# Gated linear attention with a gated projection: 64-token halves with stacked heads, a packed state, and a convolution on TensorE for two of six chunks

## The chip, the cores and the metric

The kernel runs on one core of one Trainium2 chip. Its time is the device time of one execution in microseconds (us), and a smaller number is better. TensorE (PE) multiplies matrices into PSUM; the profile lists its weight loads apart, as PEld. VectorE (DVE), ScalarE (ACT) and GpSimd (POOL) do the elementwise work. SyncE (SP) issues the transfers. PSUM has eight banks, each of 512 float32 on every one of 128 partitions.

## The reference

Two stages follow each other. The first is a linear attention with a decay of its own for each channel, with batch 4, 8 heads, 768 tokens and head dimension 48. The second is a causal convolution with 5 taps over the result, a sigmoid of it as a gate, and two projections of 384 by 384.

```python
f = 1.0 / (1.0 + np.exp(-f_logit))
for t in range(S):
    state = f[:, :, t, :, None] * state + np.einsum('bhd,bhe->bhde', k[:, :, t], v[:, :, t])
    y[:, :, t] = np.einsum('bhd,bhde->bhe', q[:, :, t], state)
# x = y with the heads side by side: [4, 768, 384]
for k in range(5):
    gate_pre += conv_w[k][None, None, :] * xp[:, k:k + S, :]    # xp: x after four rows of zeros
out = (1 / (1 + np.exp(-gate_pre))) * (x @ w_val) @ w_out
```

## The kernel before

The 768 tokens are cut into six chunks of 128. Two heads make a pair, which lies on partitions 0 to 47 and 64 to 111, with channels on partitions and tokens along the free dimension; 4 batches times 4 pairs are 16 columns ("bp") of a chunk.

For each chunk, `pexp` and `pln` (ACT) make the negative logarithm of the decay, `scan` (DVE) sums it along the chunk, and `exp1` and `exp2` (ACT) give the decay products E1 and their inverses E2. `pmulq` and `pmulk` (DVE) scale q and k by them. Then, per batch:

- `scores` (line 282): products of k and q, 128 by 128 tokens for each of eight heads, into the PSUM tile `aps`.
- `mask` (line 289): DVE multiplies all of `aps` with a triangle of ones, 128 by 1024 elements, into `asb`.
- `ktrans` and `kevac`: PE transposes k, and ACT copies it to `ksb`.
- `apply` (line 302): y of one batch into `xps`, from the state and q and from v and the masked scores. The output is split into strips of 32 channels, which run side by side on four strips of the array.
- `xevac`: ACT copies y into `XF`, behind the last four tokens of the chunk before (`halo`).
- `dstate`: the products of k and v, into `dps`. Per half of the batches `stadd` (DVE) adds them to the state, `stmul` (POOL) multiplies it with the decay over the chunk, and `stcopy` (ACT, two copies) writes it as two blocks of a diagonal into `st`, which `apply` reads.

For each chunk's projections, `msplit` (ACT) and `mlow` (DVE) split y into two parts of reduced precision. `mlast` (ACT) multiplies y with the fifth tap, and four `mconv` steps (DVE) per block of 128 channels add the other taps, each over 128 by 512 elements. `gate` (ACT) is the sigmoid. `mval` (nine products per block) makes x times w_val, `mmul` (DVE) multiplies with the gate, `mhigh` (ACT) and `mrest` (DVE) split the product, `mout` (nine products) makes the output, and `mstore` copies and stores it. The last chunk's projections are done as two halves of the batches, numbered 5 and 6.

The weights come as 64-bit numbers. `weight` rebuilds float32 from their bits on POOL, ACT and DVE, in several steps each.

The order of the work is written out by hand: `PROGRAM` (lines 37 to 100) lists the pieces, and each engine does its instructions in the order in which they are written (class `Ordered`, line 103). Loads and stores go through SP's queue in the order of the program; a load whose buffer is still being read waits there, and everything behind it waits too. "busy" pieces are products of zeros that nobody reads. After the program a flag tells whether every chunk's decay stayed in range; if not, a general branch does everything anew. It isn't taken here.

In the profile nearly all instructions have line 113, since `Ordered` issues them; the groups are told apart by their tiles. `mps` are the projections' two PSUM banks, `e` the decay products, `gt` the gate, and `rg` and `re` are buffers used again for parts of projections' operands.

Of the kernel before, what the change touches and what calls it, by code (L numbers as in the profile page):

```python
# [21 lines left out]
C = 128  # L22
NC = S // C
BP = B * NP
KT = 5
HALO = KT - 1
NM = DM // 128
#: a chunk's decay products have to stay above this for q * e and k / e to be formed apart
RANGE = 2.0**-58
# [3 lines left out]
WHOLE = [(0, BP)]  # L33
# [3 lines left out]
PROGRAM = """  # L37
halo 0; loadf 0 0; loadf 0 1; busy 10; loadq 0 1; loadq 0 0; loadk 0 0; loadv 0 0; pexp 0 0; loadk 0 1; loadq 0 2;
pln 0 0; loadf 1 0; scan 0 0; loadv 0 1; pexp 0 1; busy 4; loadk 0 2; exp2 0 0; pln 0 1; wload 0; exp1 0 0; busy 4;
loadk 1 0; pmulk 0 0; pexp 0 2; loadq 1 0; pmulq 0 0; ktrans 0 0; loadv 0 2; scan 0 1; pln 0 2; scores 0 0; exp2 0 1;  # L40
scan 0 2; wload 1; exp1 0 1; busy 4; kevac 0 0; pmulq 0 1; exp2 0 2; dstate 0 0; pmulk 0 1; busy 4; exp1 0 2;
mask 0 0; loadv 1 0; ktrans 0 1; loadf 2 0; okc 0; kevac 0 1; pmulq 0 2; scores 0 1; pexp 1 0; weight 0; pmulk 0 2;
apply 0 0; pln 1 0; mask 0 1; loadf 3 0; loadk 2 0; dstate 0 1; wload 2; ktrans 0 2; scores 0 2; kevac 0 2; scan 1 0;
xevac 0 0; stadd 0 0; exp2 1 0; ktrans 0 3; mask 0 2; apply 0 1; kevac 0 3; pmulk 1 0; scores 0 3; stcopy 0 0;
scan 1 1; xevac 0 1; exp1 1 0; ktrans 1 0; loadk 2 1; mask 0 3; apply 0 2; exp2 1 1; loadq 2 0; pmulq 1 0; exp1 1 1;
apply 0 3; loadv 2 0; weight 1; weight 0; xevac 0 2; weight 0; pmulq 1 1; scores 1 0; xevac 0 3; weight 1; halo 1;
msplit 0; weight 1; loadq 2 1; weight 1; dstate 0 2; mask 1 0; dstate 0 3; kevac 1 0; ktrans 1 1; weight 0; stadd 0 1;
scores 1 1; kevac 1 1; pmulk 1 1; loadv 2 1; pexp 2 0; weight 0; weight 1; dstate 1 1; weight 1; apply 1 0; okc 1;
mask 1 1; weight 1; loadf 4 0; pln 2 0; weight 1; mlow 0; weight 3; ktrans 1 2; loadk 3 0; scores 1 2; xevac 1 0;
stcopy 0 1; scan 2 0; apply 1 1; mask 1 2; exp2 2 0; exp1 2 0; weight 0; scan 2 1; weight 2; scores 1 3; loadq 3 0;  # L50
mlast 0 0; pmulk 2 0; xevac 1 1; weight 2; exp2 2 1; mconv 0 0 0; dstate 1 0; mask 1 3; apply 1 2; loadv 3 0;
kevac 1 2; exp1 2 1; pmulq 2 0; ktrans 1 3; pmulq 2 1; scores 2 0; loadk 3 1; kevac 1 3; xevac 1 2; mconv 0 0 1;
weight 3; mlast 0 1; stadd 1 0; ktrans 2 0; weight 2; mlast 0 2; dstate 1 2; stmul 1 0; weight 3; dstate 1 3;
weight 3; stcopy 1 0; apply 1 3; weight 2; mask 2 0; kevac 2 0; stadd 1 1; okc 2; scores 2 1; loadv 3 1; weight 2;
xevac 1 3; stmul 1 1; pmulk 2 1; loadq 3 1; stcopy 1 1; mconv 0 2 0; ktrans 2 1; pexp 3 0; dstate 2 0; loadk 4 0;
weight 2; apply 2 0; weight 3; mask 2 1; kevac 2 1; loadf 5 0; weight 2; mconv 0 1 0; pln 3 0; dstate 2 1; weight 2;
mconv 0 1 1; ktrans 2 2; apply 2 1; weight 4; mconv 0 1 2; kevac 2 2; stadd 2 0; weight 3; stmul 2 0; mconv 0 0 2;
weight 3; dstate 2 2; loadq 4 0; stcopy 2 0; scan 3 0; weight 3; scores 2 2; loadv 4 0; weight 5; mconv 0 0 3;
exp2 3 0; mval 0 0; mconv 0 1 3; gate 0 0; mconv 0 2 1; mconv 0 2 2; mval 0 1; mask 2 2; exp1 3 0; mmul 0 0;
ktrans 2 3; scan 3 1; mval 0 2; weight 4; weight 4; exp2 3 1; mconv 0 2 3; exp1 3 1; scores 2 3; pmulq 3 0; halo 2;  # L60
xevac 2 0; pmulk 3 0; kevac 2 3; gate 0 2; apply 2 2; loadk 4 1; mask 2 3; pmulq 3 1; xevac 2 1; dstate 2 3; weight 5;
gate 0 1; scores 3 0; weight 5; xevac 2 2; stadd 2 1; weight 5; stmul 2 1; weight 4; ktrans 3 0; weight 4; apply 2 3;
pexp 4 0; mask 3 0; weight 4; pmulk 3 1; scores 3 1; loadv 4 1; loadq 4 1; mmul 0 1; kevac 3 0; mmul 0 2; weight 4;
ktrans 3 1; pln 4 0; weight 5; weight 4; dstate 3 0; loadk 5 0; weight 5; apply 3 0; mask 3 1; weight 6; weight 5;
scan 4 0; weight 5; weight 6; scores 3 2; kevac 3 1; weight 6; xevac 2 3; exp2 4 0; weight 6; weight 6; apply 3 1;
exp1 4 0; weight 6; mask 3 2; mhigh 0 1; mhigh 0 0; mrest 0 1; dstate 3 1; loadq 5 0; weight 6; mrest 0 0; scores 3 3;
mhigh 0 2; loadv 5 0; weight 6; mlast 1 0; mrest 0 2; mlast 1 1; pmulk 4 0; mout 0 1; msplit 1; mconv 1 0 0;
# [577 lines left out]
```

## Time and profile before

| what | value |
|---|---|
| median of 3 runs | 220.92 us (220.72 to 226.4) |
| span of the profiled execution | 227.6 us |
| ACT busy in that span | 144.0 us, 63% |
| POOL busy in that span | 32.4 us, 14% |
| moved by transfers | 29.54 MB, 130 GB/s on average |
| granted TensorE clock, mean | 0.921 of full |

The profiled execution's span runs from its first to its last instruction. It is 6.7 us longer than the median of the runs.

In a group's row, the line, the engine and the operation come first, then what it writes and reads, its shapes and the number of instructions; behind the bar stand the busy time in us, the mean duration of one in ns, and the engine's idle time just before these instructions, with what ended it. Instructions of one engine overlap a little, so busy time divided by the count is somewhat less than the mean of one. A float32 product is two instructions on TensorE, and each of them has a weight load.

In a row of the timeline or of the chain, the start and the length are in us from the span's start, and merged instructions are counted at the end. The length of merged products includes the whole of the last one, and products overlap.

### The profile page before, as it was taken

The numbers are of one execution on the slowest core, as the hardware profiler recorded it, in microseconds if no ns is written. First come the engines' busy times: TensorE is split into PE (matmuls) and PEld (weight loads), VectorE is DVE, ScalarE is ACT, GpSimd is POOL, SyncE is SP. The second block draws the span as 40 slices with busy tenths as digits, with TensorE's granted clock in tenths as the row PEclk, the third lists the DMA queues.
The fourth block names the chain that finished last, engine by engine and source line by source line (L and its number), as shares of the span: only waits on it lengthen the run. The fifth ranks groups of instructions, "written<-read, shape, count | busy, mean of one in ns | idle before, by whom it ended". The sixth has DMA issues, their size and how long they took to land.

```text
span 227.6 us, 5654 instructions
## 1 busy us (share of the span) xinstructions
PE 184.2 (81%) x2437; PEld 148.5 (65%) x2438; DVE 191.7 (84%) x251; ACT 144.0 (63%) x226; POOL 32.4 (14%) x37
## 2 busy tenths in 40 slices
PE   7298689649198847775999987979879999999990
PEld 3156568438087736665787875767867788889880
DVE  5395989497499999999997999997799999998800
ACT  4677764686249298967639998553941858553630
POOL 4001011200044842240115100001200000000000
PEclk9959959976979999998599999979999999999998
DMA  6999999999959902244023050120000012111241
GB/s 190 280 254 268 333 336 278 238 239 258 240 129 278 250 15 84 81 164 143 21 92 128 3 164 0 49 95 0 4 3 0 1 49 79 62 50 42 103 152 37
DMA packets 9183, 29.54 MB, mean 130 GB/s; under 512 B 1200, under 2 KB 2224, under 8 KB 8112
## 3 DMA queue, kind: packets, MB, share of 16 engines
q1 hardware_dynamic: 9152, 29.12, 44.5%
q8 instruction: 21, 0.34, 0.6%
q14 instruction: 10, 0.08, 0.1%
HBM read 24.39 MB, written 4.72 MB: 128 GB/s over the span
## 4 chain that ended last, share of the span: by engine, by line
DVE 33%; PE 27%; DMA 24%; ACT 9%; issue 3%; SPq 2%; DVEq 0%; ACTq 0%
PE mps L113 19%; DMA qb<-in_q 10%; DVE gt L113 10%; DMA vb<-in_v 9%; DVE e L113 6%; DMA fb<-in_f 5%; DVE asb L113 5%; ACT e L113 3%; PE aps L113 3%; DVE qb L113 2%; DVE cb L113 2%; PE xps L113 2%; DVE ca L113 2%; DVE kb L113 2%; SPq L178 2%
## 5 line engine op out<-in xcount | busy, mean ns | idle before, releaser
L113 ACT ACTIVATE e<-e 112x1024 f32<-112x1024 f32 (+3 forms) x40 | 39.9, 1003 | 15.0 <-DVE e L113 14.6
L113 DVE SCALAR_TENSOR_TENSOR gt<-xf,cws,gt 128x512 f32<-128x512 f32 x60 | 45.2, 772 | 0.6
L113 PE MATMUL aps<-qb,kb 48*128 48x128 f32 x384 | 31.5, 310 | 13.3 <-DVE asb L113 11.9
L113 PE MATMUL xps<-asb,vb 128*32 128x128 f32 x768 | 38.2, 293 | 1.1 <-DMA vb<-in_v 0.7
L113 PEld LDWEIGHTS aps<-qb,kb 48*128 48x128 f32 x384 | 26.6, 210 | 19.0 <-DVE asb L113 14.2
L113 PE MATMUL xps<-qb,st 112*32 112x128 f32 x480 | 31.7, 287 | 4.7 <-issue 2.9
L113 PEld LDWEIGHTS xps<-asb,vb 128*32 128x32 f32 x768 | 32.8, 119 | 2.6 <-DMA vb<-in_v 1.0
L113 DVE TENSOR_TENSOR_SCAN e<-keep,e 112x1024 f32<-112x1024 bf16 (+1 forms) x13 | 28.7, 2218 | 5.2 <-ACT e L113 5.0
L113 PE MATMUL mps<-rg,woH 128*128 128x512 f32 (+1 forms) x102 | 32.3, 401 | 0.3 <-DVE gt L113 0.3
L113 DVE TENSOR_TENSOR asb<-aps,tri 128x1024 f32<-128x1024 f32 x24 | 29.1, 1213 | 0.0
L113 PEld LDWEIGHTS xps<-qb,st 112*32 112x32 f32 x480 | 22.2, 114 | 7.4 <-issue 3.9
L113 PEld LDWEIGHTS mps<-rg,woH 128*128 128x128 f32 x102 | 19.1, 199 | 4.6 <-DVE gt L113 0.5
L113 PE MATMUL mps<-xH,wvH 128*128 128x512 f32 x45 | 19.2, 428 | 3.1 <-DVE gt L113 2.9
L113 PE MATMUL mps<-rg,woL 128*128 128x512 f32 (+1 forms) x51 | 20.1, 395 | 0.0
L113 DVE TENSOR_TENSOR kb<-kb,e 112x1024 f32<-112x1024 f32 (+1 forms) x13 | 15.4, 1184 | 5.2 <-DMA kb<-in_k 5.2
L113 PE MATMUL mps<-xL,wvH 128*128 128x512 f32 x45 | 18.5, 410 | 0.9 <-DVE xL L113 0.9
L351 POOL TENSOR_TENSOR ss<-u,e 112x384 f32<-112x384 f32 x8 | 9.4, 1173 | 67.2 <-DVE u L113 63.3
L113 DVE TENSOR_TENSOR qb<-qb,e 112x1024 f32<-112x1024 f32 (+1 forms) x13 | 14.7, 1130 | 4.6 <-DMA qb<-in_q 4.6
L113 PE MATMUL mps<-xH,wvL 128*128 128x512 f32 x45 | 18.5, 411 | 0.0
L113 PE MATMUL dps<-vb,ksb 128*48 128x48 f32 x320 | 11.7, 226 | 7.6 <-DVE u L113 5.1
L113 PEld LDWEIGHTS dps<-vb,ksb 128*48 128x48 f32 x320 | 9.7, 137 | 11.5 <-DVE u L113 5.3
L113 ACT ACTIVATE e<-fb 112x2048 f32<-112x2048 f32 (+2 forms) x8 | 11.8, 1481 | 8.3 <-DMA fb<-in_f 8.2
(107 smaller groups left out, 301.8 us busy)
## 6 DMA issues: line engine op xcount, KB each, us to landing
fb<-in_f SPq DMA_DIRECT2D x5, 896.0 KB, 19.1
qb<-in_q SPq DMA_DIRECT2D x9, 448.0 KB, 8.1
kb<-in_k SPq DMA_DIRECT2D x9, 448.0 KB, 11.6
vb<-in_v SPq DMA_DIRECT2D x9, 448.0 KB, 9.4
out<-osb SPq DMA_DIRECT2D x15, 256.0 KB, 2.0
raww<-in_wv SPq DMA_DIRECT2D x1, 1152.0 KB, 19.8
raww<-in_wo SPq DMA_DIRECT2D x1, 1152.0 KB, 26.7
kb<-in_k SPq DMA_DIRECT2D x1, 896.0 KB, 13.5
```

Of the source, the lines that this page charges most:

```text
L113: ins = emit(*a, **kw)
L178: nc.sync.dma_start(dst[c % NB][: src.shape[1], x0:x1], src[c, :, x0:x1])
L351: nc.gpsimd.tensor_tensor(out=ss[:, HS[h]], in0=U[h][:], in1=decay(c, h), op=ALU.mult)
```

## The change

The layout of a chunk's attention changes, the state is kept in another form, the convolution of two chunks moves to TensorE, and the whole order is new.

- **Halves.** A chunk of 128 tokens is handled as two halves of 64 (u = 0, 1). Scores are made only inside each half, as 64 by 64 squares. What the second half takes from the first comes through a state at the middle of the chunk (`MID`). Pieces work on two batches at a time (h = 0, 1), so there are 12 of each kind for 24.
- **Stacked heads.** The two heads of a pair have their tokens on different halves of the 128 partitions: masked scores, transposed k and v hold one head's 64 tokens on partitions 0 to 63 and the other's on 64 to 127. v is laid out with 160 columns for 112, with zeros between, and the inputs have 128 partitions for 112.
- **Packed state.** The state holds 64 columns per pair: for one head, and for the other, the parts that go to a shared strip of 32 channels lie in the same columns. `stmid` adds the first half's products to it (DVE, out of PSUM), and `stend` the second half's; `stmul` multiplies in place. `stadd` and `stcopy` go.
- **PSUM.** Six banks are three pairs that transposes, states, scores and y take in turn; when none of these is left to come, the banks pass to the projections.
- **Four taps in one product.** For chunks 3 and 4, `xload` copies y into `X4`, 32 channels at a time, four times, each shifted by one token; `mfour` multiplies with a matrix of four diagonals, and `mfifth` adds the fifth tap out of PSUM. `mlast` and `mconv` of those chunks go.
- **Loads.** f is loaded straight into E1, where `pexp` works in place; the buffers `fb` go. Stores are pieces of their own (`out`).

The diff, cut to its core:

```diff
-    qb = [mp.tile([112, BP, C], F32, name=f"qb{i}") for i in range(NB)]
-    vb = [mp.tile([C, BP, 112], F32, name=f"vb{i}") for i in range(NB)]
+    qb = [mp.tile([128, BP, C], F32, name=f"qb{i}") for i in range(NB)]
+    vb = [mp.tile([C, BP, VA + VB], F32, name=f"vb{i}", tag=f"vb{i}") for i in range(NB)]
+    pairs = [ps.tile([128, 2, 512], F32, name=f"pair{i}") for i in range(3)]
...
+    for t in pairs:
+        DVE.memset(t[32:64], 0.0)
...
+            DVE.tensor_tensor(out=W4[:].rearrange("p m g i -> p (m g) i"),
+                              in0=diag[:].unsqueeze(1).to_broadcast([128, 4 * NM, 32]),
+                              in1=cws[:, NM * KT :].unsqueeze(2).to_broadcast([128, 4 * NM, 32]), op=ALU.mult)
...
     def pexp(c, x0, x1, n):
-        act(LNEXP, E1[c % NB][:112, x0:x1], fb[c % NB][:112, x0:x1], AF.Exp, scale=-1.0, accum_out=sums[:, c, n : n + 1])
+        e = E1[c % NB][:112, x0:x1]
+        act(LNEXP, e, e, AF.Exp, scale=-1.0, accum_out=sums[:, c, n : n + 1])
...
+    def pair(*key):
+        held[key] = spare.pop(0)
+        uses[0] -= 1
+        return held[key]
+
+    def done(*key):
+        spare.append(held.pop(key))
+        while len(spare) > uses[0]:
+            t = spare.pop(0)
+            free.extend([t[:, 0], t[:, 1]])
+
+    def ktrans(c, h):
+        t = pair("k", c, h)
+        for i in range(HP + 1):
+            for s in range(2):
+                at = h * KH + (i * C if s == 0 else i % HP * C + HC)
+                PE.transpose(t[:, s, i * D : i * D + D], kb[c % NB][rows(s), at : at + C], ident[rows(s), rows(s)])
+
+    def dstate(c, h):
+        t, ks = pair("d", c, h), KSB[slot(c, h)]
+        for i in range(HP):
+            vt = vb[c % NB][:, h * HP + i]
+            for u in range(2 if c < NC - 1 else 1):
+                for s in range(2):
+                    r = slice(HC, C) if s == u else slice(0, HC)
...
+                    PE.matmul(t[rows(s), u, i * HC : i * HC + HC], ks[r, s, i + (u if s == 0 else 0)], vr, start=True,
+                              stop=True, tile_position=(r.start, s * HC))
+
+    def stmid(c, h):
+        t = held["d", c, h][:112, 0].rearrange("p (a e) -> p a e", e=HC)
+        DVE.tensor_tensor(out=MID[:, HS[h]], in0=ST[c % 2][:, HS[h]], in1=t, op=ALU.add)
...
+    def stend(c, h):
+        t = held["d", c, h][:112, 1].rearrange("p (a e) -> p a e", e=HC)
+        DVE.tensor_tensor(out=ST[(c + 1) % 2][:, HS[h]], in0=MID[:, HS[h]], in1=t, op=ALU.add)
+        done("d", c, h)
+
+    def stmul(c, h):
+        s = ST[(c + 1) % 2][:, HS[h]]
+        nc.gpsimd.tensor_tensor(out=s, in0=s, in1=E1[c % NB][:112, HS[h], C - 1 : C].to_broadcast([112, HP, HC]),
+                                op=ALU.mult)
+
+    def scores(c, h):
+        t, qt = pair("s", c, h), qb[c % NB]
+        kt = kview(c, h * HP, (h + 1) * HP)
+        for i in range(HP):
+            for u in range(2):
+                w = slice(u * HC, u * HC + HC)
+                for s in range(2):
+                    at = HC if s == u else 0
+                    PE.matmul(t[at : at + HC, u, i * HC : i * HC + HC], kt[rows(s), i, w],
+                              qt[rows(s), h * HP + i, w], start=True, stop=True, tile_position=(s * 64, at))
+
+    def mask(c, h):
+        DVE.tensor_tensor(out=ASB[slot(c, h)][:], in0=held["s", c, h][:].rearrange("p u (a t) -> p u a t", t=HC),
+                          in1=tri[:].unsqueeze(1).unsqueeze(1).to_broadcast([C, 2, HP, HC]), op=ALU.mult)
+        done("s", c, h)
+
+    def apply(c, h):
+        t, qt, at_, st, vt = pair("x", c, h), qb[c % NB], ASB[slot(c, h)], ST[c % 2], vb[c % NB]
...
+                    for s in range(2):
+                        if n == "s":
+                            r = rows(s)
+                            lhs, rhs = (MID if u else st)[r, bp, 32:64], qt[r, bp, w]
+                        else:
+                            r = slice(s * HC, s * HC + HC)
+                            lhs, rhs = vt[r, bp, VA + 32 :], at_[r, 1, i]
+                        PE.matmul(to(b, 2 * s, u, z), lhs, rhs, start=(b == 0 and kind == (("s", 0 if c else 1))),
+                                  stop=False, tile_position=(s * HC, z * 32))
...
+                ops = [(1, 0, st[:, bp, 0:32], qt[:112, bp, 0:HC])] if c else []
+                ops += [(1, 1, MID[:, bp, 0:32], qt[:112, bp, HC:]), (1, 1, vt[:, bp, VA : VA + 32], at_[:, 1, i])]
+                ops += [(g, 0, vt[:, bp, at : at + 32], at_[:, 0, i]) for g, at in ((0, 32), (1, 0), (2, 64))]
...
+                    PE.matmul(to(b, g, u, z), lhs, rhs, start=False, stop=(b == 1 and n >= -1), tile_position=(0, z * 32))
...
+    def xload(n, j):
+        src = XF[n % 2]
+        size = B * TH - j
+        for g in range(4):
+            nc.sync.dma_start(X4[j * 32 : j * 32 + 32, :, g].rearrange("p m b t -> p m (b t)")[:, :, 0:size],
+                              src[g * 32 : g * 32 + 32].rearrange("p m b t -> p m (b t)")[:, :, j:])
+
+    def mfour(w, m, bank):
+        w["pc", m] = bank
+        for g in range(4):
+            PE.matmul(bank[g * 32 : g * 32 + 32, : w["n"]], W4[:, m, g], X4[:, m, g, w["b"], 0:C], start=True, stop=True,
+                      tile_position=(0, g * 32))
+
+    def mfifth(w, m):
+        DVE.scalar_tensor_tensor(out=w["gt"][:, m], in0=w["xf"][:, m, w["b"], HALO:],
+                                 scalar=cws[:, m * KT + HALO : m * KT + KT],
+                                 in1=w["pc", m][:, : w["n"]].rearrange("p (b t) -> p b t", t=C), op0=ALU.mult, op1=ALU.add)
```

Of the new order, the loads of the start and the pieces behind the last mask are those that the prediction speaks of. The loads come as `loadf 0 0; wload 0; loadf 0 1; loadf 1 0; loadk 0 2; wload 1; loadk 0 1; loadk 0 0; loadq 0 0; loadv 0 1; loadv 0 2; loadq 0 1; loadq 0 2; loadv 0 0; wload 2; loadq 1 1; loadq 1 0; loadk 1 1; loadk 1 0; loadf 2 0; loadk 2 0; loadv 1 1; loadk 3 1; loadv 2 1; loadk 2 1; loadq 2 0; loadv 1 0`. Behind `mask 5 1` PE has `mval 3` (two blocks), `mval 5 1`, `apply 5 1`, `mfour 4` (three), and then the other products of `mout 3`, `mval 4`, `mval 5`, `mout 5`, `mval 6`, `mout 4` and `mout 6`. The "busy" pieces of the start stay (ten products), and the 16 in the pieces behind them go.

More of the change, by code (lines that the diff above doesn't have):

```diff
@@ L33 @@
 WHOLE = [(0, BP)]
+FOUR = (3, 4)
 PROGRAM = """
[L38 to L66, printed above, removed]
@@ L502, in gla_moe @@
     N2 = NM * 2 * C
-    proj, late, held, free, stored = {}, {}, {}, list(mps), []
-    ap2 = [flat(aps[:, n]) for n in range(2)]
-    banks = {("mval", last): [*ap2, flat(kps)], ("mout", last): [None, None, ap2[0]],
-             ("mval", NC): [dpb, *[flat(x) for x in xps]], ("mout", NC): [ap2[1], flat(kps), dpb]}
+    proj, late, stored, bufs = {}, {}, [], {}
     def retag(tag, n):
```

402 lines of the change are left out of this document (223 added, 179 removed).

## The prediction

> **What bounds the kernel now.** I read the page's busy shares and slices first, to see which engine is full where, then the busy time by stage, then the chain of waits for the hand-over points, and last the groups of instructions for prices.
>
> ```profile
> span 227.6 us, 5654 instructions
> PE 184.2 (81%) x2437; PEld 148.5 (65%) x2438; DVE 191.7 (84%) x251; ACT 144.0 (63%) x226; POOL 32.4 (14%) x37
> PE   7298689649198847775999987979879999999990
> DVE  5395989497499999999997999997799999998800
> DMA  6999999999959902244023050120000012111241
> ```
>
> DVE is the fullest engine. Its row has gaps in the first ten slices, where the DMA row is full, and is at nine almost throughout from slice 12 on; PE is full only from slice 32 on. That makes three stages, and the stage table gives them numbers (columns: busy time of PE, PEld, DVE, ACT, POOL with counts, granted clock, DMA share, GB/s):
>
> ```profile
> 0.00:60.00 60.00, 43.06 (x597) 31.30 (x598) 42.77 (x47) 39.25 (x58) 6.62 (x17) 0.83 0.99 266
> 60.00:176.00 116.00, 95.92 (x1435) 78.44 (x1436) 110.90 (x132) 78.05 (x114) 25.61 (x19) 0.94 0.30 89
> 180.00:222.00 42.00, 41.45 (x330) 35.88 (x330) 34.20 (x67) 24.14 (x52) 0.00 (x0) 1.00 0.20 73
> ```
>
> The chain of waits (start, length, what) says what ends last in each:
>
> ```profile
> 37.15 22.95 DMA qb<-in_q
> 60.22 1.23 DVE qb L113
> ...
> 180.02 6.57 PE mps L113 x27
> 186.59 3.21 PE xps L113 x112
> 189.80 2.29 PE mps L113 x9
> 192.09 1.06 PE aps L113 x9
> ...
> 221.38 0.37 ACT fb L113
> ```
>
> And DVE's timeline has the last causal mask:
>
> ```profile
> 180.67 1.21 DVE L113 TENSOR_TENSOR asb<-aps,tri 128x1024 f32<-128x1024 f32 x1
> ```
>
> Start, 0 to 60: transfers end last (DMA share 0.99), and DVE idles 17.2 us. Middle, 60 to about 180: DVE idles 5.1 of 116 us, so whatever is taken from DVE here comes off the time. Tail, 180 to 221.4: PE without a break (41.45 of 42), so DVE work removed here is worth nothing. That mask ended at 181.9; behind it PE still has everything of the last products. I use that mask as the hand-over: span = end of the last mask + PE work listed behind it + 6.2 us to the end.
>
> **The change part by part.** Prices, from the groups (busy time, mean ns of one, idle before):
>
> ```profile
> L113 DVE SCALAR_TENSOR_TENSOR gt<-xf,cws,gt 128x512 f32<-128x512 f32 x60 | 45.2, 772 | 0.6
> L113 DVE TENSOR_TENSOR asb<-aps,tri 128x1024 f32<-128x1024 f32 x24 | 29.1, 1213 | 0.0
> L113 DVE TENSOR_TENSOR u<-ss,dps 112x384 f32<-112x384 f32 x8 | 4.4, 546 | 0.0
> L113 DVE TENSOR_TENSOR gt<-mps,gt 128x512 f32<-128x512 f32 x15 | 10.2, 685 | 4.5 <-ACT gt L113 2.6 <-PE mps L113 1.8
> L113 ACT COPY st<-ss 48x384 f32<-48x384 f32 x20 | 10.2, 509 | 6.7 <-POOL ss L351 6.5
> L351 POOL TENSOR_TENSOR ss<-u,e 112x384 f32<-112x384 f32 x8 | 9.4, 1173 | 67.2 <-DVE u L113 63.3
> L113 ACT ACTIVATE gt<-xf,cws 128x512 f32<-128x512 f32 x15 | 10.6, 720 | 4.0 <-DVE rg L113 4.0
> L113 ACT ACT_TABLE_LOAD x8 | 10.3, 1283 | 0.9 <-PEq L636 0.8
> ```
>
> DVE up to the last mask, busy time divided by count. Masks: a chunk's 128x128 score squares become two 64x64 ones, and twelve masks of the same 128x1024 stand for 24: 12 x 1.21 = -14.5 us. Convolution: chunk 3's twelve taps (12 x 0.753) become three fifth-tap steps of the same shape (3 x 0.753): -6.8. Chunk 4 saves as much, but behind the last mask, under PE: nothing. State: ten adds of 0.55 go, 22 come (12 to the mid state, 10 to the end state), 112x512 with one operand in PSUM, for which the nearest row is gt<-mps at 0.68: +15.0 - 5.5 = +9.5. Three gate products of chunk 3 are written behind the last mask instead of ahead: -2.0. The wider tap weights, the table W4 and clearing three PSUM pairs add about 1.6, partly under the first load. Sum -12.2. Everything else of DVE (scans, scaling of q and k, weights, mlow) keeps size and count.
>
> ACT: 20 state copies go (-10.2), six mlast go (6 x 0.7 = -4.3), the evacuations keep their elements, and the program's order has ten table loads for eight (+2.6). About -12 in all, worth nothing on time: ACT has 38 us free in the middle. POOL: stmul grows by a third (1.17 to some 1.56) and runs ten times for eight, but the two ACT copies behind it go, so the state reaches the next chunk no later (1.56 against 1.17 + 0.51). This is hidden under other work of DVE; if that cover is gone, 0.4 us per half.
>
> PE, in instructions (each float32 product is two). Paces:
>
> ```profile
> 173.44 1.16 PE L113 MATMUL aps<-qb,kb 48*128 48x128 f32 x16
> 104.05 0.56 PE L113 MATMUL dps<-vb,ksb 128*48 128x48 f32 x16
> 117.60 0.40 PE kps L113 x4
> 46.51 0.30 PE L113 MATMUL xps<-qb,st 112*32 112x128 f32 x1 [2.92 <-issue]
> L113 PE MATMUL aps<-qb,kb 48*128 48x128 f32 x384 | 31.5, 310 | 13.3 <-DVE asb L113 11.9
> L113 PE MATMUL dps<-vb,ksb 128*48 128x48 f32 x320 | 11.7, 226 | 7.6 <-DVE u L113 5.1 <-ACT ksb L113 1.3 <-issue 1.1
> ```
>
> Subtracting one duration: scores go at (1.16 - 0.31)/15 = 57 ns on two strips of the array, 114 per strip; dstate at (0.56 - 0.23)/15 = 22 on two strips, 44 each; xps at 3.21/112 = 28.7 on four, 115 each. So a strip takes 44 ns for 48 columns and 114 for 128: an estimate of 59 for 64. Now: 24 x 16 x 57 ns = 21.9 (scores) + 20 x 16 x 22 = 7.0 + 20 x 0.40 = 8.0 (transposes) + 1248 x 28.7 = 35.8, together 73 us. After, if four 64x64 squares run side by side: scores 12 x 16 rounds x 59 = 11.3; dstate the same, 11.3; transposes 216, bounded by 0.10 (alone) and 0.05 (two strips): 0.05 taken, since scores show two row strips side by side, 10.8; apply 2.1 per half-chunk and less in chunk 0, 24.6; the four-tap products 6 x 0.9 = 5.4. Together 63, so -10. In the start and the middle this is hidden under DVE and gains nothing by itself. Only the tail counts. Behind the last mask PE had 39.0 us of list; the new order has 40.6 (two value blocks of chunk 3, nine-product blocks at 2.1 and 1.06 as in the chain, one apply, three four-tap products): +1.6.
>
> Transfers. q, k and f go from 896 to 1024 KB per chunk, v from 896 to 1280: +21%. Sixteen 32-partition copies make up X4 per chunk, 3.2 MB, in chunks 3 and 4.
>
> ```profile
> fb<-in_f SPq DMA_DIRECT2D x5, 896.0 KB, 19.1
> 1.29 0.41 SPq L178
> DVE kb L113 <- DMA kb<-in_k: 5.2, 2, 3.6
> DVE qb L113 <- DMA qb<-in_q: 4.6, 1, 4.6
> L113 ACT ACTIVATE e<-e 112x2048 f32<-112x2048 f32 x5 | 9.6, 1913 | 0.1
> ```
>
> The copies cost SP 16 x 0.41 = 6.6 us of issue and, at the 266 GB/s of the start, 12 us of transfer; DMA share is 0.30 and 0.20 in the stages where they fall, and the list puts 12 us of PE work between the last copies of chunk 3 and their product. Behind them on SP stand the last loads of chunk 5 and the stores. I cost them at nothing; uncovered, 3 to 8 us.
>
> The start: on SP's queue, 12.6 MB stand up to the q load that landed at 60.1 (two whole chunks of 3584 KB, weights of 2304, f of chunks 2 and 3, k and half of q of chunk 2): 0.21 MB/us. In the new order chunk 1 is complete after 9.8 MB, at about 46 us, and DVE needs some 44 us of work for that point, so it is less late. But f is now loaded in place into E1, so chunk 2's f starts only when chunk 0's stmul is over; 4.8 us of transfer and two passes of 1.9 us on ACT follow before the scan can run. DVE will stand there, I estimate for 5 us. Bounds: -10 (the gap at 55.6 to 60.2 and the earlier ones gone) to +8 (this wait whole); I take -3, nearer to the bytes. New waits in the middle (three PSUM pairs shared by transposes, states, scores and y; mid state before the second half): 0 to +18 (1.5 us for each of 12 halves); I take +1, since the rows show DVE waiting only 1.8 us for PE.
>
> Sum: -12.2 + 1.6 - 3 + 1 = -12.6. The profiled execution spans 227.6 us; the median is 220.92, 6.7 us less, and I carry the difference over unscaled: a span of 215, a time of 208 us.
>
> **The rivals.** (1) PE can't take more, smaller products (the slow side). Place: the middle. PE idles 20 us there, of which 8 are left once the stage is 12 shorter; about 0.8 of the 3896 attention instructions fall in it. The point that decides: at 20 ns per instruction (3896 x 20 = 78, + 5.4, is 10 above today's 73) PE takes over from DVE. The rows never show an average under 22 ns over a run of products: at 22 (dstate) it is 91 us, +18 x 0.8 - 8 = +6.5, so 214.5; at 28.7 (xps) 117, +27, so 235. For it: this floor, and the 2.92 us in which PE stood in mid-apply for nothing shown while transfers were at 0.99. Against it: both paces also follow from strip time alone, and 22 came with half the strips idle. The Trainium skill, TensorE: Matmul & The Clock Gate, Back-to-back issue gap, gives 1 to 64 columns one price of about 60 cycles, a 25 ns floor; by it, an estimate, 3896 x 25 + 5.4 = 103 us of attention and 224 us. The dstate row's 22 lies a little under that floor. The Trainium skill's TensorEngine Tiling (Array Packing), Gotcha 1: PSUM Pressure, says that row tiles can't use one PSUM bank at the same time; the new scores and dstate write one bank from both row halves in turn, which by that rule would double both (an estimate of 218 us). No trace here shows such a pair.
>
> (2) The saving goes back as waits: DVE stands for a PSUM pair or a landing. For: 48 uses share three pairs, and k, v and E1 are reloaded only after their last reader. Against: DVE waited 5 us in 116 before. At the upper bound of 18 for 1, 225; from 215.
>
> (3) The start gains more: all of the 10 us and no wait for f: 200 to 203.
>
> **How the numbers follow.** Forecast 0.48 (203 to 216), rival 1 0.20 (214 to 235), rival 2 0.17 (215 to 228), rival 3 0.15 (196 to 203). A difference under 2%, 4.4 us, is about what a measurement here can't tell from none. Faster (under 216.5): 0.47 + 0.14 + 0.02 = 0.63. Within: 0.07 + 0.11 + 0.01 = 0.19. Slower (over 225.3): 0.13 + 0.05 = 0.18. The range is 197 to 226, leaving out rival 1's upper half and a little of 3; the forecast's own is 203 to 216.
>
> **What would show it.** Twelve masks and about 36 fewer long taps in DVE's groups, busy time near 175; DVE at nine from slice 9 or 10 on; the last mask ended near 168, and PE unbroken for 41 us behind it. Rival 1: PE's row at nine in the middle while DVE drops, and xps products over 20 ns apart. Rival 2: DVE idle before stmid, stend, pmul or scan, released by PE or DMA. The X4 copies: PE waiting ahead of the four-tap products. I am wrong if the last mask ends later than 172, or if PE has holes behind it.

## The result, and the profile after

| what | before | after |
|---|---|---|
| median, same chip (lowest to highest) | 221.12 us (220.72 to 226.4) | 253.3 us (251.81 to 254.37) |
| span of the profiled execution | 227.6 us | 252.7 us |

The ratio is 1.148 with a 95% interval of 1.141 to 1.156: the change makes the kernel 32 us slower, and the forecast was 208. In some executions a kernel takes over 1.5% longer than in its fastest; the ratios leave these out, the medians do not. First the page of the kernel after, busy shares and slices (PEclk is the granted TensorE clock in tenths):

```profile
span 252.7 us, 9517 instructions
PE 183.0 (72%) x4334; PEld 147.5 (58%) x4334; DVE 179.3 (71%) x235; ACT 133.9 (53%) x194; POOL 43.5 (17%) x51
PE   7015776797986985469937991397899897969880
DVE  7599996999994699449983995068694665642730
PEclk9999999569657999658975999579999999999997
DMA  6999959433492356511864999200089810111031
```

DVE does less, 179.3 us for 191.7, and PE's busy time hardly moves. But no engine is full in the middle any more: from slice 12 on, DVE and PE both have holes where DVE was at nine before. The windows of the kernel after, cut where its last mask ends (columns as in the stage table before):

```profile
0.00:60.00 60.00, 36.81 (x956) 28.83 (x960) 52.75 (x65) 36.59 (x51) 20.29 (x37) 0.91 0.76 282
60.00:195.00 135.00, 100.71 (x2961) 81.89 (x2950) 98.19 (x113) 75.78 (x100) 23.22 (x14) 0.82 0.52 147
195.00:247.00 52.00, 45.47 (x435) 36.74 (x433) 28.37 (x59) 21.57 (x45) 0.00 (x0) 1.00 0.25 76
```

And DVE's timeline of the kernel after at that mask:

```profile
193.61 1.22 DVE L113 TENSOR_TENSOR asb<-pair,tri 128x1024 f32<-128x1024 f32 x1
```

It ends at 194.8; I had said 168. DVE stands idle for 135 - 98.2 = 36.8 us in the middle, for 5.1 before. Behind the mask come 57.9 us to the end of the span, for 46.8 forecast. What does DVE wait for? The waits of the kernel after (us in total, times, longest us):

```profile
PEld pair L113 <- issue: 42.4, 34, 10.6
...
PE pair L113 <- issue: 20.7, 12, 4.9
DVE gt L113 <- PE mps L113: 17.8, 5, 11.4
...
ACT osb L113 <- DMA out<-osb: 13.4, 1, 13.4
...
PE mps L113 <- ACT osb L113: 7.7, 1, 7.7
```

DVE waits for PE; and PE, in the first rows, waits for nothing that the profile shows. Its timeline has such a stop in the middle of a y product:

```profile
98.31 0.63 PE L113 MATMUL pair<-asb,vb 128*32 128x64 f32 x32
...
98.98 0.51 PE L113 MATMUL pair<-asb,vb 128*32 128x64 f32 x23
104.40 0.53 PE L113 MATMUL pair<-asb,vb 128*32 128x64 f32 x9 [4.90 <-issue]
```

The same 32 products, with operands that lie ready, are cut at the 23rd for 4.9 us. While it runs, PE is quick: 32 in 0.63 us. What remains as a suspect is the arrival of the instructions themselves. The page's DMA section counts the instruction fetches (queue q8: packets, MB, share), before:

```profile
q8 instruction: 21, 0.34, 0.6%
```

and after:

```profile
q8 instruction: 36, 0.59, 1.0%
```

A packet is 16 KB. PE has 2437 products and as many weight loads before (4875 instructions), 8668 after: about 256 to a packet, with two or so left over. Bytes are nothing here; the question was whether each packet is a stop. The trace has more on it: in the kernel after PE has eleven stops of 0.4 us or more for which the profile names nothing that ended them ("issue", below: without a releaser), 21.9 us together. The products between one and the next number 256, 891, 255, 256, 508, 128, 254, 128, 384 and 125. These are multiples of 128, less a few records that the trace lacks, and 128 products with their weight loads are 256 instructions. Ahead of each stop's end, by 2.2 to 3.1 us, a 16 KB packet of this queue starts.

### The profile page after: what moved, and what is told of

It is laid out like the page before. It is cut to its first block, busy times and chain, and to the rows that moved or that the text cites. A ratio compares the mean times of both kernels' runs of the same rounds, so it can differ in the third digit from the quotient of the medians.

```text
span 252.7 us, 9517 instructions
## 1 busy us (share of the span) xinstructions
PE 183.0 (72%) x4334; PEld 147.5 (58%) x4334; DVE 179.3 (71%) x235; ACT 133.9 (53%) x194; POOL 43.5 (17%) x51
## 5 line engine op out<-in xcount | busy, mean ns | idle before, releaser
L113 PE MATMUL pair<-asb,vb 128*32 128x64 f32 (+1 forms) x1152 | 31.1, 249 | 11.1 <-issue 11.1
L113 DVE TENSOR_TENSOR_SCAN e<-keep,e 112x1024 f32<-112x1024 bf16 (+1 forms) x13 | 29.6, 2296 | 3.6 <-ACT e L113 3.1
L113 PEld LDWEIGHTS pair<-asb,vb 128*32 128x32 f32 (+1 forms) x1152 | 24.3, 126 | 11.9 <-issue 11.9
L361 POOL TENSOR_TENSOR st<-st,e 112x512 f32<-112x512 f32 x10 | 19.9, 1992 | 59.3 <-DVE st L113 48.1
L113 DVE SCALAR_TENSOR_TENSOR gt<-xf,cws,gt 128x512 f32<-128x512 f32 x36 | 27.3, 784 | 2.3 <-ACT gt L113 2.3
L113 PE MATMUL pair<-ident,kb 48*128 48x48 f32 x216 | 11.9, 260 | 21.1 <-DVE kb L113 17.1
L113 PE MATMUL pair<-qb,kb 48*64 48x64 f32 x768 | 20.2, 274 | 8.0 <-issue 4.3
L113 PEld LDWEIGHTS pair<-qb,kb 48*64 48x64 f32 x768 | 18.0, 183 | 11.4 <-issue 5.8
L113 PE MATMUL pair<-vb,ksb 64*48 64x64 f32 x704 | 18.9, 269 | 4.3 <-issue 3.4
L113 PE MATMUL pair<-qb,mid 48*32 48x64 f32 (+1 forms) x576 | 19.0, 249 | 1.7 <-DVE mid L113 1.2
L113 PEld LDWEIGHTS pair<-vb,ksb 64*48 64x48 f32 x704 | 16.8, 162 | 5.6 <-issue 4.3
L113 PE MATMUL pair<-rg,woH 128*128 128x512 f32 (+1 forms) x48 | 14.7, 382 | 4.9 <-ACT rg L113 1.9
L113 ACT CAST rg<-gt 128x512 fp32r<-128x512 f32 x15 | 9.1, 622 | 14.9 <-DVE gt L113 14.9
L113 DVE TENSOR_TENSOR qb<-qb,e 112x1024 f32<-112x1024 f32 (+1 forms) x13 | 16.8, 1295 | 0.0
L113 DVE TENSOR_TENSOR mid<-st,pair 112x512 f32<-112x512 f32 x12 | 8.2, 682 | 11.5 <-PE pair L113 11.4
```

The lines of the kernel that those rows point to most:

```text
L113: ins = emit(*a, **kw)
L361: nc.gpsimd.tensor_tensor(out=s, in0=s, in1=E1[c % NB][:112, HS[h], C - 1 : C].to_broadcast([112, HP, HC]), op=ALU.mult)
```

## The experiments

Two theories stood against each other. **Supply**: PE's instructions arrive in blocks of 256, and short products use a block up faster than the next one comes. **Order**: the hand-written order, the three shared PSUM pairs and the queue of stores make the waits, and the stops are a by-product. Below, an "instruction pair" is one product instruction with its weight load; a block holds 128 pairs.

### Products alone, and beside transfers

Two small programs hold nothing of the kernel: 1024 float32 products of 64 columns on four strips of 32 channels, then 512 of 128 columns, on constants (two pairs each), with zeros as output. The second has 40 loads of 896 KB beside them.

```diff
+PHASES = [(64, 1024), (128, 512)]
+LOADS = 40
...
+    for n in range(LOADS):
+        nc.sync.dma_start(bufs[n % 4][:], (q, k, f)[n % 3][n % NC])
...
+    for cols, count in PHASES:
+        for n in range(count):
+            s = n % 4
+            PE.matmul(acc[0][s * 32 : s * 32 + 32, 0:cols], w[:, s], x[:, 0:cols], start=True, stop=True,
+                      tile_position=(0, s * 32))
```

> Only streams of products on four strips, no attention and no projections: 1024 float32 products of 64 columns (4096 instructions with their weight loads), then 512 of 128 columns. Supply theory (PE's instructions arrive in blocks of 256, and a block takes some us to come): the 64-column phase runs no faster than a block in about 3.7 us, so some 59 us, with idle stretches of PE inside the phase and nothing that it waits for; the 128-column phase, 8 blocks, about 30 us. Rival, the order of the work alone costs the time: products go at strip pace, 15 ns per instruction pair and 30 us for the first phase, 29 us for the second, without holes.

> The same streams while 40 loads of 896 KB keep the transfers full. Supply theory: the blocks come later beside full transfers, so the holes grow and the 64-column phase takes 60 to 90 us. Rival: as without the loads.

They took 100.4 and 187.5 us. PE's timeline in the 64-column part, without transfers:

```profile
23.67 1.99 PE L45 MATMUL acc<-x,w 128*32 128x64 f32 x128 [1.46 <-issue]
27.40 1.99 PE L45 MATMUL acc<-x,w 128*32 128x64 f32 x128 [1.74 <-issue]
```

and with them:

```profile
45.73 3.24 PE L45 MATMUL acc<-x,w 128*32 128x64 f32 x128 [5.30 <-issue]
54.66 3.64 PE L45 MATMUL acc<-x,w 128*32 128x64 f32 x128 [5.70 <-issue]
```

Each run is exactly 128 pairs, one block, and before each stands a stop. The windows give the pace; without transfers (64 columns, then 128):

```profile
12.00:68.00 56.00, 31.16 (x1841) 28.97 (x1844) 0.00 (x0) 0.00 (x0) 0.94 0.08 29
70.00:98.00 28.00, 26.91 (x964) 25.98 (x953) 0.23 (x1) 0.00 (x0) 1.00 0.02 5
```

and beside them:

```profile
20.00:160.00 140.00, 62.50 (x2069) 59.45 (x2072) 0.00 (x0) 0.00 (x0) 0.64 1.02 245
```

Alone, the 64-column part goes at 56/1841 = 30 ns a pair, no faster than 128 columns at 28/964 = 29, although 128 of them run off in 1.99 us, at most 15.5 ns each. Beside full transfers it is 140/2069 = 68 ns. Supply in short: a block in about 3.7 us when the transfer engines are free, in about 9 when they are full. Of the 9 us, 5.3 to 5.7 are the stop; the run itself is also slower, 3.2 to 3.6 us for 2.0, at a granted clock of 0.64 for 0.94. The block matches the Trainium skill, Runtime: NRT & Kernel Launch, Instruction fetch mechanics (16 KB, 256 instructions); that page also says that the fetch is hidden because instructions are dispatched more slowly than they come, and these rows differ: PE stops before every block shown.

### Fewer instructions, then as many again

The kernel after, with score, state and y products that read only the upper 16 bits of their operands, in one pass for two (a lower precision). Everything else of the program stays. Then the same, with every such product issued as two of half the columns: the same work, and as many instructions as in the kernel after.

```diff
+    def up(t):
+        b = t.bitcast(BF16)
+        return b[:, 1::2] if len(b.shape) == 2 else b[:, :, 1::2]
+    def product(o, w, x, **kw):
+        w, x = up(w), up(x)
+        PE.matmul(o, w, x, **kw)
...
-                    PE.matmul(t[at : at + HC, u, i * HC : i * HC + HC], kt[rows(s), i, w],
+                    product(t[at : at + HC, u, i * HC : i * HC + HC], kt[rows(s), i, w],
```

> The changed kernel, where scores, state and y products read only the upper 16 bits of their operands: one instruction pair in place of two, 1840 pairs fewer, same order, same waits, same transfers. Supply theory: PE's holes inside pieces (about 21 us in the changed kernel) go, and most of that comes off the time: 225 to 235 us. Order theory: DVE and the in-order queues set the time, so 245 to 253 us.

> As the one before, but each such product is issued as two of 32 columns, so PE has as many instructions as the changed kernel while its arithmetic per product stays a quarter. Supply theory: the holes come back, time back within 8 us of the changed kernel's 253. Order theory, or PE's arithmetic as the cause: the same time as the one before.

219.5 us (0.996 of before, 0.991 to 1.001) with 21 blocks, and 249.1 (1.116, 1.098 to 1.134) with 36. The second computes what the first does, with the same banks and transfers, and PE, DVE and ACT have the same order; 15 blocks more are 29.6 us by the medians and 26.6 by the ratios. In the first, the waits have no row in which PE's products stand without a releaser. In the second they have this one:

```profile
PE pair L113 <- issue: 41.3, 17, 5.1
```

One thing differs besides. SP's transfers don't keep strictly to the order of the program in the changed kernels (of the kernel before it was said that they do), and the two traces have them in different orders: in the first, one store of chunk 1 goes ahead of the last four copies of chunk 3, in the second all three stores stand behind all 16. PE waits 4.2 us for an output buffer in the first and 6.9 in the second, so about 3 us of the difference may come from there. The stages of the first, around its last mask at 159.1:

```profile
60.00:159.00 99.00, 72.39 (x1594) 54.10 (x1592) 92.39 (x106) 71.30 (x94) 28.91 (x13) 0.78 0.63 188
159.00:214.00 55.00, 46.91 (x338) 38.07 (x336) 28.61 (x60) 22.62 (x46) 0.00 (x0) 0.94 0.27 78
```

and of the second:

```profile
60.00:188.00 128.00, 85.21 (x2911) 67.06 (x2911) 94.52 (x110) 73.17 (x96) 25.82 (x13) 0.72 0.52 152
188.00:242.00 54.00, 47.08 (x437) 38.44 (x436) 28.98 (x60) 22.63 (x47) 0.00 (x0) 0.97 0.27 76
```

The whole difference lies ahead of the last mask; in the last stretch, with wide products, both are alike. That carries supply as the main cause, and rejects the order of PE, DVE and ACT: with it, the shared pairs and the lower precision, the kernel takes no longer than the kernel before. One thing stays open: PE is also busy 12.8 us longer in the middle of the second (85.2 for 72.4), so part of the difference may be a cost of each product by itself.

### How much of it: the y products alone

```diff
...
-                    PE.matmul(to(b, g, u, z), lhs, rhs, start=False, stop=(b == 1 and n >= -1), tile_position=(0, z * 32))
+                    product(to(b, g, u, z), lhs, rhs, start=False, stop=(b == 1 and n >= -1), tile_position=(0, z * 32))
```

> The changed kernel with upper-half products for y alone (1104 instruction pairs less, 8.6 of the 14 blocks that all of them save); scores and states stay float32. If each block costs about the same wherever it falls (33.8 us for 15 blocks): 253.3 - 8.6 x 2.25, so 232 to 237, with 27 or 28 blocks. Rival (PE's slack takes up the first blocks saved or the last ones; only the y products, which PE does in the longest unbroken runs, pay): 222 to 229. If it is the state and score products that pay: 243 to 251.

233.1 us (1.062, 1.054 to 1.070), with 27 blocks. Nine blocks less are 20.2 us; the next six, down to 21, are 13.6: about 2.25 us a block in both steps. These steps also halve the work of the products; the pair above, where the work stays, has 1.8 to 2.0.

### The copies into X4

The stores of chunk 1 stand on SP behind the copies. SP's timeline in the kernel after (L457 is `xload`, L659 `out`):

```profile
137.32 17.07 SPq L457 DMA_DIRECT2D x<-xf  x16
154.84 7.41 SPq L659 DMA_DIRECT2D out<-osb  x3
```

`PROGRAM` has chunk 1's first store behind four of the copies and the other two behind eight; here all three stand behind all 16. ACT waits 13.4 us for an output buffer, PE 7.7 for ACT, and DVE 11.4 for PE: the rows of the waits above. One kernel issues chunk 1's stores from ACT's queue, one takes the copies away (POOL fills X4 with zeros once, so the gate lacks the four taps).

```diff
-out 1 2;
+out 1 2 1;
...
-out 1 1; out 1 0;
+out 1 1 1; out 1 0 1;
```

```diff
     def xload(n, j):
...
-        for g in range(4):
...
+        if n == 3 and j == 3:
+            nc.gpsimd.memset(X4[:], 0.0)
```

> The changed kernel, with the three stores of chunk 1 issued from ACT's queue for SP's, so that they do not stand behind the copies of y into X4. Store-wait theory: ACT's 13.4 us wait for a free output buffer goes, and with it PE's gap of 7.8 and DVE's of 11.4 us near 154; 4 to 8 us less, 245 to 249. Rival (the copies themselves fill the transfer queues, so the stores land as late from any queue; or PE's supply takes the time up): 252 to 254.

> The changed kernel without the copies of y into X4, whose place is filled with zeros once by POOL: the four taps of chunks 3 and 4 are left out of the gate, and every product and instruction stays. If the copies cost by slowing the supply of PE's instructions (a block of 256 took 9 us beside full transfers, 3.5 us alone) and by holding up chunk 1's stores: PE's stops between 125 and 165 shrink, 8 to 12 us less, 241 to 246, with as many blocks fetched (36). Rival (the stores were worth 2 us with the queue changed, and the other stops lie elsewhere): 249 to 253.

Another queue gave 251.3 (1.139, 1.128 to 1.150), which can't be told from 253.3. But it did not take the wait away. ACT stands there 10.8 us for an output buffer, for 13.4, first until a copy has landed:

```profile
154.27 0.59 ACT L115 COPY osb<-mps 128x512 f32<-128x512 f32 x1 [5.94 <-DMA x<-xf]
159.70 0.59 ACT L115 COPY osb<-mps 128x512 f32<-128x512 f32 x1 [4.84 <-DMA out<-osb]
```

Without the copies it is 239.6 (1.089, 1.078 to 1.100): 13.7 us, somewhat more than expected, with 35 blocks. The same 40 us of both kernels, after:

```profile
125.00:165.00 40.00, 24.74 (x601) 20.32 (x591) 24.08 (x29) 19.87 (x26) 2.22 (x1) 0.77 0.70 166
```

and without copies:

```profile
125.00:165.00 40.00, 34.14 (x1028) 28.04 (x1016) 33.27 (x39) 23.44 (x35) 5.52 (x4) 0.87 0.24 84
```

With a DMA share of 0.24 for 0.70, PE gets 1028 products done for 601. Is that supply, or the stores? The same product, the first of a block of chunk 2's values, with the copies and without:

```profile
161.95 0.80 PE L113 MATMUL mps<-xH,wvH 128*128 128x512 f32 x1 [7.75 <-ACT osb L113]
```

```profile
152.84 0.40 PE L113 MATMUL mps<-xH,wvH 128*128 128x512 f32 x1
```

The block of values before it begins at 150.07 and 150.63, so up to there the copies cost nothing. Here they have cost 9.1 us: 7.75 behind the store, and a stop of 1.6 without a releaser. Over the whole kernel, stops without a releaser on PE are 22.3 us with the copies and 20.7 without. So most of the 13.7 us is the wait for the stores, and only a few us are supply. The same removal in the upper-half kernel, where supply hardly binds:

> The changed kernel with upper-half products and without the copies of y into X4 (zeros in their place, so the four taps of chunks 3 and 4 are left out of the gate). In float32 the copies cost 13.7 us. If they cost it by making the blocks of instructions come later, little of it is left with 15 blocks fewer, only the wait for chunk 1's stores (4 us of DVE near 130): 214 to 218. If they cost it by the stores and by the wait for the copies themselves, whatever PE has to fetch: 205 to 211.

216.3 us (0.981, 0.970 to 0.992), so there the copies cost 3.2 us. That fits the stores, too: PE stands 4.2 us for the output buffer there, for 7.7. No run keeps the copies and takes the whole wait away, so this part is read and not tested. With chunk 1's stores on ACT's queue in place of that:

> The changed kernel with upper-half products and chunk 1's stores issued from ACT's queue. In float32 that queue was worth 2 us. With PE fed, the wait for a free output buffer (PE's gap of 4.2 and DVE's of 4.1 us near 130) ends DVE's work directly: 215.5 to 218, below the kernel before. If the stores land as late beside the copies from any queue: 219 to 221.

218.8 (0.993, 0.988 to 0.997): the fastest of these kernels that leaves nothing out, at the lower precision, and less than one per cent ahead of the kernel before.

### The same dose in the kernel before

Every y product of the kernel before as two of 64 columns (1248 pairs more), and its score, state and y products from the upper halves (a lower precision):

```diff
-        for r in zip(*lanes):
-            for z, (m, w, x, start, stop) in enumerate(r):
-                PE.matmul(x_[z * 32 : z * 32 + 32, m], w, x, start=start, stop=stop, tile_position=(0, z * 32))
+        for t in (slice(0, 64), slice(64, 128)):
+            for r in zip(*lanes):
+                for z, (m, w, x, start, stop) in enumerate(r):
+                    PE.matmul(x_[z * 32 : z * 32 + 32, m, t], w, x[:, t], start=start, stop=stop, tile_position=(0, z * 32))
```

> The kernel before, whose y products (apply) are each issued as two of 64 columns: 1248 more instruction pairs, 2496 instructions, about ten more blocks of 256, with the same layout, order, transfers and work of the other engines. Supply theory: two 64-column strips take as long as one of 128, but PE stands once in every 256 instructions; at the 2 us per block that the two forms of the changed kernel differ by (29.6 us for 15 blocks) 20 us more, so 235 to 245, with about 31 blocks fetched and the longest stops of PE in the first 60 us, where the transfers are full. Rival (instructions come as fast as the array takes them; the changed kernel's time is in its order or its shared PSUM pairs): the same strips at 59 ns for 114, so 221 to 226.

> The kernel before, whose score, state and y products read the upper 16 bits of their operands (one instruction pair each for two): about 976 pairs, 1952 instructions, 7 to 8 blocks less. Supply theory: PE had slack in the middle, which DVE bounds, so fewer blocks are worth little there; the one y product group and the scores of the tail get shorter by 2 to 3 us, and stops of PE in the start go: 214 to 220. It stands beside the changed kernel with the same products, 219.5: if the old layout is as fast or faster there, the halves and their order are worth nothing even when supply does not bind. Rival (the new order is worth its 12 us of DVE once PE is fed): the old layout stays at 219 to 221, and 219.5 is then limited by something else in the changed kernel.

The split gave 1.036 (1.018 to 1.054), some 8 us for ten blocks: supply in sign, but 0.8 us a block, where I had expected 2. The middle of this kernel shows why it could be so:

```profile
60.00:184.00 124.00, 107.92 (x2489) 90.32 (x2481) 118.05 (x142) 86.61 (x129) 25.36 (x20) 0.94 0.27 84
```

With a DMA share of 0.27 a block comes at nearly the pace of free engines, and 2489 pairs at 30 ns are 75 of 124 us. So the price of a block isn't fixed. The small programs show that it depends on the transfers beside it; here PE also had time to spare, and the two were not separated.

The upper halves made the kernel before slower, 227.1 (1.029, 1.020 to 1.038), with 13 blocks for 21; I had expected 214 to 220. Its granted clock is 0.757, for 0.915 to 0.946 in runs of the kernel before beside it. Here PE with less to do was granted a lower clock; that this makes the 6 us was not shown. Hence "new against old layout, with PE fed" (219.5 to 227.1) is not a clean comparison.

### What the four-tap product is worth

In the changed kernel, DVE and ACT add the taps as before, without copies:

```diff
-FOUR = (3, 4)
+FOUR = ()
...
-mfour 3 2; mfifth 3 2;
+mlast 3 2; mconv 3 2 0; mconv 3 2 1; mconv 3 2 2; mconv 3 2 3;
```

> The changed kernel with upper-half products, and with the four taps of chunks 3 and 4 added by DVE and ACT as before: no copies into X4, no table W4, no four-tap products. If the four-tap product is worth what I summed (6.8 us of DVE before the last mask, chunk 4's under PE) 219.5 becomes 224 to 228. If what the copies cost (stores behind them on SP: PE stands 4.2, DVE 4.1 us near 130) is as much as they save: 217 to 222.

> The changed kernel with upper-half products, and the four taps of chunks 3 and 4 added by DVE, all at the places of the fifth taps (the run before had the first two earlier, where they overwrote a gate still needed: its time stands, its values do not). Nothing is copied into X4. If the four-tap product is worth what I summed before the last mask and nothing behind it: 224 to 228 for 219.5, the mask 7 us later and the same stretch behind it. If it pays behind the mask too (PE there waits for DVE): 228 to 233, with the stretch behind the mask 4 us or more longer.

> The changed kernel in float32, the four taps of chunks 3 and 4 added by DVE at the places of the fifth taps, nothing copied. With upper-half products this took 237.0 for 219.5. If the two costs simply add (the four-tap product is worth 17 us whatever PE's supply): 268 to 272. If the copies' 13.7 us are given back, and DVE's 18 taps before and 24 half the way into the last stretch cost about as much: 250 to 257, so that the four-tap product was worth nothing in the changed kernel.

With upper halves 229.6 (1.041, 1.032 to 1.050; taps partly earlier, where they overwrite a gate of the chunk before that is still read) and 237.0 (1.082, 1.073 to 1.092); in float32 263.0 (1.192, 1.175 to 1.209) for 253.3. So by the whole time the four-tap product was worth about 10 us in the float32 kernel, in spite of its copies. But all of this came behind the last mask: in float32 that mask ends at 188.6 without it and at 194.8 with it, so ahead of the mask it cost 6.2 us. With upper halves the mask ends 4.5 us later without it. The last stretch without it, upper halves:

```profile
164.00:229.00 65.00, 45.21 (x311) 37.24 (x309) 35.10 (x67) 23.73 (x48) 0.00 (x0) 0.84 0.11 39
```

65 us for 55, with PE hardly less busy: there PE stands up to 10.9 us at a time until DVE is through. The bunched taps are a poor order for it, so 10 is an upper value.

Moved alone into the kernel before (two of chunk 3's blocks, order kept), it did not pay:

```diff
+xload 3 0; xload 3 1; xload 3 2; xload 3 3;
...
-mlast 3 0; mconv 3 0 0; apply 5 0; mconv 3 0 1;
+mfour 3 0; apply 5 0; mfifth 3 0; mfour 3 2;
```

> The kernel before, its layout and order kept, with the four-tap product for two of the three blocks of chunk 3 (copies into X4 behind the chunk's last y, 1.4 MB written, then mfour and mfifth where the last product of chunk 2 has passed). If a tap removed from DVE in the stage that DVE bounds comes off the time: six taps of 0.75 us less, two products of 0.9 us more on PE where it has slack, 0.5 us for the table, so 216.5 to 218 beside 221.3. Rival (the copies hold up the loads of chunk 5 behind them on SP, or slow PE's supply; or the wait for the copies takes the place of the taps): 220 to 224.

223.4 (1.012, 1.004 to 1.021): DVE's busy time fell by 3.3 us (191.7 to 188.4), and the time did not. Whether the copies or the wait for the product took it back is open.

## Why the prediction was wrong

**The step that failed** is the sentence "In the start and the middle this is hidden under DVE and gains nothing by itself", and the pace behind it, "an estimate of 59 for 64". As a pace of the array the estimate was good: 59 ns on four strips is 14.8 ns an instruction, and the runs above go at under 15.5 once they are fed. But I took the array's pace for that of PE. Instructions come at one pair in about 27 to 30 ns at best and in 68 beside full transfers, so halving a product's columns saves nothing and doubling the number of products costs. In the middle PE got 2961 pairs in 135 us, 46 ns each, at a DMA share of 0.52, between the two measured ends. Before, it was 1435 pairs in 116 us, 81 ns each, more than the supply takes at either end. The price is 29.6 us between the two upper-half kernels (26.6 by the ratios, about 3 of it perhaps from the stores), and 33.8 from the first of them to the kernel after; there the last mask moves by 35.7.

**Rival 1** was right in kind, and had 0.20. I priced it by rows of the old kernel (20 to 28.7 ns, at most 235 us), and these rows couldn't show the supply beside transfers. The one row that did, the 2.92 us stop in the middle of `apply` at a DMA share of 0.99, I quoted as evidence for it and gave no price. The rival's sign, PE at nine in the middle with products over 20 ns apart, did not come: PE was busy 100.7 of 135 us, quick between its stops. The 25 ns that I took from the Trainium skill, TensorE: Matmul & The Clock Gate, Back-to-back issue gap, is not a floor here: 32 products ran in 0.63 us. That its mean lies near the supply's free pace says nothing, since the mechanism is another. The other rule, from the Trainium skill, TensorEngine Tiling (Array Packing), Gotcha 1: PSUM Pressure, doesn't bind either; by it two row halves on one bank would take twice 14.8 ns, and the scores' row of the kernel after, where row halves write one bank in turn, has at most 17.9 ns each:

```profile
177.79 1.00 PE L113 MATMUL pair<-qb,kb 48*64 48x64 f32 x56
```

The rival's 218 us for that rule doesn't follow from its own rows either: scores and dstate doubled make 63 + 22.6 = 85.6, and by its formula (12.6 x 0.8 - 8) that is 210.

**DVE's sum** (-12.2) held in the groups that change, and fell short in all. DVE's busy time up to the last mask is 159.4 before and 150.7 after, 8.6 less (11.1 in the upper-half kernel). Its groups after:

```profile
L113 DVE SCALAR_TENSOR_TENSOR gt<-xf,cws,gt 128x512 f32<-128x512 f32 x36 | 27.3, 784 | 2.3 <-ACT gt L113 2.3
...
L113 DVE TENSOR_TENSOR asb<-pair,tri 128x1024 f32<-128x1024 f32 x12 | 14.5, 1216 | 1.8 <-PE pair L113 1.8
...
L113 DVE TENSOR_TENSOR mid<-st,pair 112x512 f32<-112x512 f32 x12 | 8.2, 682 | 11.5 <-PE pair L113 11.4
...
L113 DVE TENSOR_TENSOR st<-mid,pair 112x512 f32<-112x512 f32 x10 | 6.7, 679 | 0.0
```

Masks 14.5 less as said, state adds 14.9 for 15.0, 24 long taps gone. What was to keep its size did not quite: the scaling of q took 16.8 us for 14.7, the scans 29.6 for 28.7. With PE fed, the last mask ended at 159.1, 9 us ahead of the 168 that I forecast: the mechanism was there, and was covered.

**The start** (-3) was better than the term: DVE idles 7.2 us in the first 60 for 17.2, the lower bound of -10. The wait for f in E1 that I put against it (5 us) is not seen.

**The waits** (+1, bounds 0 to 18) were exceeded: 36.8 us of DVE idle in the middle. 11.4 of it is the wait behind chunk 1's stores. Most of the rest I read as the supply seen from DVE: in the upper-half kernel DVE's idle time is 99 - 92.4 = 6.6.

**The copies** (0, uncovered 3 to 8) cost 13.7. What waits behind them on SP was the right place to look, but the size was wrong: SP is at them for 17.1 us, where the 6.6 us of issue were summed, and the buffer that waits for a store behind them is what PE and DVE then stand for.

**The tail** (+1.6) was mis-sized by 11 us, and no supply is in it: the upper-half kernel has 60.6 us behind its last mask, the kernel after 57.9, and none of the eleven stops counted in the kernel after lies there. By the trace PE is busy for 45.5 us there, for the 40.6 of my list. I had missed `mout 2 1` (2.1 us), which stands ahead of `mask 5 1` in the order; the mask does not wait for it and ended ahead of it. The other 2.8 us were not traced to single products. And PE has holes of 6.5 us, such as this one in its timeline after:

```profile
210.56 0.70 PE L113 MATMUL pair<-rg,woH 128*128 128x512 f32 x2 [1.55 <-DVE gt L113]
```

Each is a product that waits for the one before it by way of DVE or ACT. No run took these holes away, so this part is read, not tested. For the same reason "Chunk 4 saves as much, but behind the last mask, under PE: nothing" doesn't hold: where PE has such holes, DVE's taps lie on the path.

So 252.7 is the forecast span of 215, with the mask later by 26.8 (9 us gained, and 35.7 lost from the upper-half kernel to this one) and the tail longer by 11. One more term was off: the forecast took 6.7 us from the span to reach the time, but the kernel after has a span 0.6 us below its median. That makes some 7 of the 45 us between 208 and 253.

## What to carry to other kernels

Count instructions as well as columns: a block of 256 that PE works off in less time than the next takes to arrive is a stop, and beside full transfers a block came two to three times as slowly (9 us for 3.7). Before cutting products smaller, divide a stage's length by its product instructions and compare with what the trace shows as a supply; a "waits for nothing shown" in the middle of a run of ready products can be that limit, above all when such stops are 128 products apart, and deserves a price. And a transfer that is "hidden" because the queue has room can still cost, by way of what stands behind it: here a store, with it a buffer, and then three engines.

## What was not expected of the hardware

- The supply of PE's instructions: a stop after every 128 pairs, one block in about 3.7 us alone and 9 us beside transfers at a share of 1.02.
- The kernel before with two fifths of its PE instructions taken away (2924 for 4875) became 2.9% slower, at a granted clock of 0.757; why is open.
- The price of splitting products differs from kernel to kernel: 0.8 us a block in the kernel before, at a DMA share of 0.27, and about 2 in the changed kernel, at 0.52.
